# A fill by load instead of a memset, and one late store shared by two queues, in a sparse attention and ELU feed-forward kernel

## The chip, the core and the metric

The kernel runs on one core of one Trainium2 chip. A core has TensorE (PE in the profile; its weight loads are PEld), VectorE (DVE), ScalarE (ACT), GpSimd (POOL) and SyncE (SP), and 16 DMA engines. Each engine works through its own list of instructions in order, and waits at an instruction until the semaphores that this one names have been reached. SP, ScalarE and GpSimd also issue DMAs. The metric is the device time of one execution in microseconds; the median of three runs of the kernel before is 307.64 us (307.57 to 308.14).

## The reference, cut to what matters

Eight batches of eight heads of 576 tokens with 64 dimensions go through masked attention; four heads have a local mask (the last 32 tokens), four a strided one (tokens at the same place modulo 32). The result, 4608 tokens of 512 features, goes through a feed-forward part with an ELU between its two products.

```python
scores = scale * np.matmul(q, k.transpose(0, 1, 3, 2))
mask_local = (rel >= 0) & (rel < stride)                       # stride = 32
mask_strided = (rel >= 0) & (pos[None, :] % stride == pos[:, None] % stride)
masks = np.stack([mask_local if h < H // 2 else mask_strided for h in range(H)], axis=0)
scores = np.where(masks[None, :, :, :], scores, -1000000000.0)
attn = np.exp(scores - np.max(scores, axis=-1, keepdims=True))
attn = attn / (np.sum(attn, axis=-1, keepdims=True) + 1e-09)
x = np.matmul(attn, v).transpose(0, 2, 1, 3).reshape(B * S, H * D)   # 4608 x 512
h = x @ w_in                                                         # 512 -> 2048
g = np.where(h > 0.0, h, np.exp(np.minimum(h, 0.0)) - 1.0)
out = g @ w_out                                                      # 2048 -> 512
```

## The kernel before, in words

Tokens are handled in a permuted order: 576 tokens are 72 places by 8 phases, so both masks become small blocks. Attention works by pairs of heads: a pair is named by batch, kind (`s` strided, `l` local) and a number, as in `0l1`. Its steps are the products of scores (`S`, L450), the exponential on ScalarE (`e`, L457), the multiplication with the mask on VectorE (`m`, L464 for strided and L470 for local pairs), the products with the values (`O`), the logarithm and the reciprocal of the sums on ScalarE (`n`, L548, and `r`, L553), and the product that writes the normalised result, transposed, into `xT` (`x`, L578, VectorE).

The feed-forward part works on nine chunks of 512 tokens. For each chunk there are 16 tiles of the first product (`L`, or its halves `a` and `b`, L605), each followed by an exponential on ScalarE (`h`, L613), a clamp (`i` on VectorE, L622, or `j` on ScalarE, L620) and the step that forms the ELU (`g`, VectorE, L633 or L631). Then four output tiles of 128 tokens follow: their products (`Z`, L639, in four parts), a copy from PSUM to SBUF (`o` on ScalarE or `q` on VectorE, L645) and the store (`t`, L657).

All of this is written out by hand: the string `ORDER` lists every step as a token, and each engine and each DMA queue gets its instructions in this order. `D` tokens issue loads from GpSimd's queue (`D.ql.3` the local queries of batch 3, `D.wo0.0` a quarter of the second weight matrix); `X` tokens issue transposing DMAs from SP's queue; `F.mk` and `F.ml` make the local mask. `w` tokens are products of zeros that fill TensorE's gaps in the first 20 us.

Around the first edit: `F.mk` runs on GpSimd two selections that form `mask_1` (L340, L343), and then the memset of rows 64 to 79 of the tile `ql1` (L346). `F.ml` runs on VectorE two copies that spread `mask_1` into the two halves of `mask_l` (L349), and a small memset (L351). In `ORDER` the tokens between and behind them are, in the neighbourhood: `F.mk r.0s0.0 ... D.wo0.0 F.ml e.0l1.0 ... c.0l0.k n.0s0.1 D.wo1.0 ... m.0l1.0 ... r.0s1.1 ... x.0s1.1 ... V.0`. Here `c.0l0.k` is the copy of transposed keys on VectorE (L426), `V.0` a copy within the value tile (L582).

`ql1` is the second buffer of the local queries; batches 3, 5 and 7 load it, 72 rows each, four loads (L239, one per head). A transposing DMA (L598) reads it in blocks of 80 rows, so its rows 72 to 79 are read too, although no product uses what comes of them. The first buffer, `ql`, has its 80 rows filled by the load of batch 0.

Around the second edit: the last tokens of `ORDER` finish chunks 8 and 7. A tile of 128 tokens is stored in two or three DMAs, because its rows cross the phase blocks in `out`. `store` takes a list of engines, SP alone by default, and its DMAs go to them by turns. The last tile (`Y` and `y` tokens, L669 and L679) is computed and stored in three pieces of 256, 128 and 128 columns; the first piece's two DMAs go from SP, those of the other two from SP and ScalarE by turns. The built program gives DMAs eight completion semaphores for the loads of GpSimd's queue and eight for the DMAs of SP's and ScalarE's queues together, and uses them in turn; a DMA's issue waits until the DMA before it on its semaphore has landed, unless an earlier wait says so already.

Of the kernel before, what the change touches and what calls it, by code (L numbers as in the profile page):

```python
# [17 lines left out]
HG = 4  # L18
NS = 8
RS = S // NS  # L20
RP = 80
# [9 lines left out]
NPE = 2  # L31
# [109 lines left out]
i.7.14 g.7.14 Z.7.2.0.6 h.7.4 i.8.8 j.7.8 Z.8.2.0.7 g.8.8 g.7.8 j.7.4 Z.8.0.0.4 g.8.10 L.8.15.1 g.7.4  # L141
Z.8.3.1.2 h.8.15 i.8.15 Z.8.0.1.4 g.8.15 Z.8.2.1.7 Z.8.1.0.5 Z.7.2.1.6 Z.8.1.1.5 Z.7.1.0.3 Z.8.1.2.5
Z.8.0.2.4 Z.7.2.2.6 Z.8.1.3.5 Z.8.0.3.4 o.8.1 Z.7.0.1.0 o.8.0 t.8.0 Z.8.3.2.2 Z.7.1.1.3 t.8.1 Z.7.1.2.3
Z.8.3.3.2 Z.7.2.3.6 o.8.3 t.8.3 Z.7.0.2.0 q.7.2 Z.7.1.3.3 t.7.2 Z.7.0.3.0 q.7.1 Z.8.2.2.7 t.7.1 q.7.0
Z.8.2.3.7 t.7.0 Y.7.3.0.6 o.8.2 t.8.2 y.7.3.0 Y.7.3.1.5 y.7.3.1 Y.7.3.2.4 y.7.3.2
"""

# [2 lines left out]
def kernel(  # L150
# [9 lines left out]
    nc = tc.nc  # L160
# [20 lines left out]
    g = [consts.tile([128, MC, CHUNK], BF16, tag=f"g{i}", name=f"g{i}") for i in range(2)]  # L181
# [10 lines left out]
    odd = {"ql": consts.tile([RP, HG * NS * D], BF16, tag="ql1", name="ql1"),  # L192
           "kl": consts.tile([LQ, HG * LB * D], BF16, tag="kl1", name="kl1")}
# [25 lines left out]
    def rawof(nm, b):  # L219
        if b == 1:  # L220
            return raw1[nm]
        return odd[nm] if b % 2 and nm in odd else raw[nm]

    def runs(x, b, h, n):

        rows = RP if (b * H + h + n - 1) * S + RP * NS <= B * H * S else RS
        return rows, bass.AP(x.tensor, x.offset + (b * H + h) * S * D,
                             [[NS * D, rows], [S * D, n], [1, NS * D]])
# [5 lines left out]
            out=rawof(nm, b)[0:rows].rearrange("p (h f) -> p h f", h=HG)[:, h0:h0 + n], in_=in_)  # L234

    def load_qloc(b):
        t = rawof("ql", b).rearrange("p (y s x d) -> p y s x d", y=2, s=NS, x=2)
        for h in range(HG):
            nc.gpsimd.dma_start(  # L239
                out=t[0:RS, h % 2, :, h // 2, :],  # L240
                in_=q[b, h].rearrange("(p s) d -> p s d", s=NS))
# [21 lines left out]
    def load(what, b, y=None):  # L263
        nm, b = what[:2], int(b)
        if y is not None:
            load_runs(nm, b, 2 * int(y), 2)
            return
        if nm == "wi":
            i = int(what[2])
            nc.gpsimd.dma_start(out=w_in_sb[:, :, i * 512:(i + 1) * 512],  # L270
                                in_=w_in_v[:, :, i * 512:(i + 1) * 512])
        elif nm == "wo":
            i = int(what[2])
            nc.gpsimd.dma_start(out=w_out_sb[:, i * 4:(i + 1) * 4, :],
                                in_=w_out_v[:, i * 4:(i + 1) * 4, :])
        elif nm == "vl":
            load_vloc(b)
        elif nm == "ql" and b >= NPE:
            load_qloc(b)
        elif nm == "kl" and b >= NPE:  # L280
            load_kloc(b)
        else:
            load_runs(nm, b)
# [5 lines left out]
    for eng, n, x in ((nc.sync, 0, q), (nc.scalar, 1, k)):  # L289
        for i in range(2):  # L290
            rows, in_ = runs(x, 0, HG, 2)
            f = NS * D // 2
            eng.dma_start(out=half(stage[0:rows, n * 4 * f:(n + 1) * 4 * f], i),
                          in_=in_[:, :, i * f:(i + 1) * f])
# [14 lines left out]
    def fill_ones(t, n):  # L309
        w = t.bitcast(F32)  # L310
        nc.vector.memset(
            w[:, 0:n * D].rearrange("p (n w d) -> p n w d", w=2, d=D // 2)[:, :, 0, :], two)
        nc.vector.memset(w[:, n * D:], two)

    def fill_vloc(t):
        fill_ones(t, HG * LB)
        nc.vector.memset(blocks(t, HG * LB)[0:PRE, 0, :], 0.0)
# [10 lines left out]
    def fill(what):  # L328
        if what == "ms":
            nc.vector.tensor_scalar(same, dist, scalar1=STRIDE // NS - 1, scalar2=None,  # L330
                                    op0=ALU.bitwise_and)
            nc.vector.tensor_scalar(eq, same, scalar1=0, scalar2=None, op0=ALU.is_equal)
            nc.vector.scalar_tensor_tensor(mask_s, dist, float(RS), eq, op0=ALU.is_ge,
                                           op1=ALU.mult)
        elif what == "vp":
            fill_ones(vs_p, HG * NS)
        elif what == "v1":
            fill_vloc(vl_t[1])
        elif what == "mk":
            nc.gpsimd.affine_select(  # L340
                mask_1, mask_1, compare_op=ALU.is_ge, fill=0.0,
                base=-1, pattern=[[-1, NS], [-NS, LN]], channel_multiplier=1)
            nc.gpsimd.affine_select(  # L343
                mask_1, mask_1, compare_op=ALU.is_ge, fill=0.0,
                base=PRE, pattern=[[1, NS], [NS, LN]], channel_multiplier=-1)
            nc.gpsimd.memset(odd["ql"][64:RP], 0.0)  # L346
        else:
            for u in range(2):
                nc.vector.tensor_copy(mask_l[:, u],  # L349
                                      mask_1.unsqueeze(2).to_broadcast([128, NS, 3, LN]))  # L350
            nc.vector.memset(mask_l[0:PRE, 0, :, 0, :], 0.0)  # L351
# [263 lines left out]
    def clamp(eng, ch, m):  # L615
        i = int(ch), int(m)
        e = tiles.pop(("he", i))
        e1 = p_he1.tile([128, CHUNK], BF16, tag="he1", name="he1")
        if eng is nc.scalar:
            nc.scalar.activation(e1, e, ACT.Relu, bias=1.0, scale=-1.0)  # L620
        else:
            eng.tensor_scalar(e1, e, scalar1=1.0, scalar2=1.0, op0=ALU.min, op1=ALU.subtract)  # L622
        tiles["he1", i] = (e1, eng is nc.scalar)
# [19 lines left out]
    def copy_o(eng, ch, kk):  # L643
        o_sb = tiles["osb", ch, kk] = p_osb.tile([128, d_model], F32, tag="osb", name="osb")
        eng(o_sb, tiles.pop(("o", int(ch), int(kk))))  # L645
# [3 lines left out]
    def store(ch, kk, engs=(nc.sync,), fs=slice(0, d_model)):  # L649
        o_sb = tiles["osb", ch, kk]  # L650
        c0 = int(ch) * CHUNK + int(kk) * 128
        c, i = c0, 0
        while c < c0 + 128:
            b, r = divmod(c, S)
            s, p = divmod(r, RS)
            n = min(RS - p, c0 + 128 - c)
            engs[i % len(engs)].dma_start(out=out_v[b, s, p:p + n, fs], in_=o_sb[c - c0:c - c0 + n, fs])  # L657
            c, i = c + n, i + 1
# [15 lines left out]
    def out_piece(ch, kk, i):  # L674
# [8 lines left out]
    run = {  # L683
        "w": warm, "K": lambda nm, x: cast(nc.vector.tensor_copy if nm == "q" else nc.scalar.copy, nm, x),
        "k": lambda nm, x: cast(nc.scalar.copy if nm == "q" else nc.vector.tensor_copy, nm, x), "T": transposes, "F": fill,
        "c": lambda *a: copy_T(nc.vector.tensor_copy, *a),
        "C": lambda *a: copy_T(nc.scalar.copy, *a),
# [2 lines left out]
        "a": lambda ch, m, bk: l1(ch, m, (2, 3), bk), "b": lambda ch, m: l1(ch, m, (0, 1)),  # L690
        "L": lambda ch, m, bk: l1(ch, m, (2, 3, 0, 1), bk), "h": exp_h,
        "i": lambda *a: clamp(nc.vector, *a), "j": lambda *a: clamp(nc.scalar, *a),
        "g": elu, "Z": l2, "t": store, "Y": l2_piece, "y": out_piece,
        "o": lambda *a: copy_o(nc.scalar.copy, *a),
        "q": lambda *a: copy_o(nc.vector.tensor_copy, *a),
    }
# [33 lines left out]
```

## Time and profile before

| | us |
|---|---|
| median of three runs | 307.64 |
| the profiled execution, as a whole | 308.06 |
| its span, from the first to the last instruction | 306.3 |
| TensorE busy (matmul) | 294.3 |
| VectorE busy | 227.3 |
| ScalarE busy | 228.6 |
| GpSimd busy | 81.7 |

The granted TensorE clock was 0.998 on the mean. The lines that follow below are taken from one execution. A line of a timeline gives the start, the duration, the engine, the line of the kernel, the operation, what it writes and reads, its shape and how many like it were merged; in brackets stands how long the engine had been idle before it, and what ended that. A line of the chain gives start, duration and what held the end of the kernel up in that time. A line of a group by source line gives least, median and greatest duration in ns. A line of waits gives who waited for what, the total in us, how often, and the longest. An engine's name with a q behind it is its queue, where DMAs are issued and semaphores are waited for.

### The profile page before, as it was taken

The page shows a single profiled execution, that of the slowest core. Times are in us where ns is not written, and L with a number is a line of the kernel's source. Part 1 is how long each engine was busy: PE and PEld are TensorE (multiplying, and loading weights), DVE is VectorE, ACT ScalarE, POOL GpSimd, SP SyncE. Part 2 cuts the span into 40 slices and gives each one's busy share as a digit, 9 for nine tenths or more (in the row PEclk, how much of TensorE's full clock was granted, in tenths as well). Part 3 has the DMA queues.
Part 4 walks back from the last instruction along what each step waited for, and adds up shares of the span by engine and source line. Part 5 has one row for each costly group of instructions (what it writes and reads, how often), then busy time and mean ns, then how long its engine had stood idle before and what let it go on. Part 6 is the DMA issues. An engine that isn't in the chain of part 4 may idle for free.

```text
span 306.3 us, 6219 instructions
## 1 busy us (share of the span) xinstructions
PE 294.3 (96%) x2299; PEld 146.8 (48%) x2339; DVE 227.3 (74%) x435; ACT 228.6 (75%) x412; POOL 81.7 (27%) x110
## 2 busy tenths in 40 slices
PE   6999999999999999999999999999999999999993
PEld 2654455445544454545544554454444544444453
DVE  6877959798779978896788878976788468894020
ACT  4778678588879888997989889978786659881110
POOL 8943336630472008530178240000000000000000
PEclk9999999999999999999999999999999999999999
DMA  8999999999999859999899599601120022000143
GB/s 164 184 206 206 207 193 166 153 196 207 169 153 168 127 118 134 162 193 159 203 149 155 65 138 167 166 26 46 37 68 0 2 68 68 2 1 0 28 150 98
DMA packets 107278, 37.59 MB, mean 123 GB/s; under 512 B 89104, under 2 KB 102768, under 8 KB 107248
## 3 DMA queue, kind: packets, MB, share of 16 engines
q0 software_dynamic: 69648, 19.43, 62.9%
q1 hardware_dynamic: 37088, 17.38, 27.8%
q10 hardware_dynamic: 512, 0.39, 0.5%
q8 instruction: 18, 0.29, 0.4%
q14 instruction: 12, 0.10, 0.1%
HBM read 39.47 MB, written 9.44 MB: 160 GB/s over the span
## 4 chain that ended last, share of the span: by engine, by line
PE 86%; DVE 6%; ACT 2%; issue 2%; DMA 2%; ACTq 0%; DVEq 0%
PE ps L639 39%; PE ps L605 36%; PE ps L450 3%; DVE g L633 2%; PE ps L520 2%; PE ps L513 2%; DVE he L622 2%; DMA g<-in_k_dram 2%; PE ps L669 1%; ACT he L613 1%; DVE mask_l L349 1%; DVE xT L578 1%; PE ps L493 0%; ACT e L457 0%; PE ps L408 0%
## 5 line engine op out<-in xcount | busy, mean ns | idle before, releaser
L639 PE MATMUL ps<-w_out_sb,g 128*128 128x512 bf16 x538 | 129.6, 379 | 2.0 <-issue 0.6
L605 PE MATMUL ps<-xT,w_in_sb 128*128 128x512 bf16 x559 | 129.4, 379 | 1.6 <-issue 0.3
L613 ACT ACTIVATE he<-ps 128x512 f32<-128x512 f32 x144 | 81.0, 597 | 22.2 <-PE ps L605 19.9
L605 PEld LDWEIGHTS <-w_in_sb 128*128 128x128 bf16 x576 | 55.0, 98 | 64.9 <-issue 1.7
L639 PEld LDWEIGHTS <-g 128*128 128x128 bf16 x560 | 51.1, 98 | 55.6 <-issue 0.6
L633 DVE TENSOR_TENSOR g<-he,ps 128x512 bf16<-128x512 bf16 x92 | 62.0, 684 | 1.9
L578 DVE TENSOR_TENSOR xT<-ps,ln 64x576 bf16<-64x576 f32 (+1 forms) x64 | 42.5, 677 | 19.7 <-ACT ln L553 18.9
L457 ACT ACTIVATE e<-ps 72x576 bf16<-72x576 f32 (+1 forms) x64 | 39.1, 647 | 13.4 <-PE ps L450 11.7
L622 DVE TENSOR_SCALAR he<-he 128x512 bf16<-128x512 f32 x92 | 40.1, 445 | 7.7 <-ACT he L613 7.0
L548 ACT ACTIVATE ln<-ps 64x576 f32<-64x576 f32 (+1 forms) x64 | 36.3, 583 | 9.8 <-PE ps L520 4.9
L631 DVE SCALAR_TENSOR_TENSOR g<-he,ps 128x512 bf16<-128x512 bf16 x52 | 34.8, 682 | 7.2 <-ACT he L620 6.9
L553 ACT ACTIVATE ln<-ln 64x576 f32<-64x576 f32 (+1 forms) x64 | 38.5, 619 | 1.2
L620 ACT ACTIVATE he<-he 128x512 bf16<-128x512 f32 x52 | 32.5, 630 | 1.6 <-DVE g L633 1.1
L645 DVE COPY osb<-ps 128x512 f32<-128x512 f32 x22 | 15.1, 685 | 16.3 <-PE ps L639 16.0
L239 POOL DMA_DIRECT2D ql<-in_q_dram x24 | 19.9, 833 | 6.8 <-DMA vl<-in_v_dram 3.1
L645 ACT COPY osb<-ps 128x512 f32<-128x512 f32 x13 | 7.6, 586 | 18.0 <-PE ps L639 14.1
L246 POOL DMA_DIRECT2D kl<-in_k_dram x24 | 17.8, 745 | 11.9 <-DMA w_out_sb<-in_moe_w_out_dram 4.0
L470 DVE TENSOR_TENSOR pm<-e,mask_l 128x576 bf16<-128x576 bf16 x32 | 14.1, 454 | 7.0 <-ACT e L457 5.4
L464 DVE TENSOR_TENSOR pm<-e,mask_s 72x576 bf16<-72x576 bf16 x32 | 14.2, 450 | 4.3 <-ACT e L457 4.1
L233 POOL DMA_DIRECT2D vs<-in_v_dram x8 | 5.2, 653 | 26.4 <-DVE vsp L585 25.2
L256 POOL DMA_DIRECT2D vl<-in_v_dram x8 | 9.6, 1195 | 8.7 <-PE ps L520 6.4
L513 PEld LDWEIGHTS <-vsp 72*128 72x128 bf16 x192 | 9.1, 98 | 5.4 <-DVE pm L464 0.3
(93 smaller groups left out, 156.1 us busy)
## 6 DMA issues: line engine op xcount, KB each, us to landing
out_dram<-osb SPq DMA_DIRECT2D x32, 144.0 KB
vl<-in_v_dram POOLq DMA_DIRECT2D x8, 288.0 KB, 8.8
w_in_sb<-in_moe_w_in_dram POOLq DMA_DIRECT2D x4, 512.0 KB, 13.0
w_out_sb<-in_moe_w_out_dram POOLq DMA_DIRECT2D x4, 512.0 KB, 16.3
kl<-in_k_dram POOLq DMA_DIRECT2D x24, 72.0 KB, 7.7
ql<-in_q_dram POOLq DMA_DIRECT2D x24, 72.0 KB, 8.8
ks<-in_k_dram POOLq DMA_DIRECT2D x5, 320.0 KB, 8.4
vs<-in_v_dram POOLq DMA_DIRECT2D x5, 320.0 KB, 8.6
```

Of the source, the lines that this page charges most:

```text
L457: nc.scalar.activation(e[0:R], tiles.pop(("S", key, u))[0:R], ACT.Exp, scale=scale)
L548: nc.scalar.activation(t, s_ps, ACT.Ln)
L553: nc.scalar.activation(t, t, ACT.Exp, scale=-1.0)
L578: nc.vector.tensor_mul(dst, o_ps, rc)
L605: nc.tensor.matmul(tiles["h", ch, m], lhsT=w_in_sb[:, c, m * 128:(m + 1) * 128], rhs=xT[:, c, ch * CHUNK:(ch + 1) * CHUNK], start=(c == 2) ...
L613: nc.scalar.activation(e, tiles["h", i[0], i[1]], ACT.Exp)
L620: nc.scalar.activation(e1, e, ACT.Relu, bias=1.0, scale=-1.0)
L622: eng.tensor_scalar(e1, e, scalar1=1.0, scalar2=1.0, op0=ALU.min, op1=ALU.subtract)
L631: nc.vector.scalar_tensor_tensor(dst, e1, -1.0, h, op0=ALU.mult, op1=ALU.max)
L633: nc.vector.tensor_tensor(dst, e1, h, op=ALU.max)
L639: nc.tensor.matmul(ops, lhsT=g[ch % 2][:, m, kk * 128:(kk + 1) * 128], rhs=w_out_sb[:, m, :], start=(m == 0), stop=(m == MC - 1), skip_gro ...
L645: eng(o_sb, tiles.pop(("o", int(ch), int(kk))))
```

## The change

The memset of `ql1` is taken out of `F.mk`. In its place the loads of `D.ql.3` begin with one more load, of eight rows by four heads from the query tensor (2 KB of float32 each), into rows 72 to 79 of `ql1`; batches 5 and 7 find them filled. Tile 8.3 is stored with the new token `u`, which gives the store SP and ScalarE by turns: its first DMA (56 rows) goes from SP, its second (72 rows) from ScalarE.

```diff
@@ -141,7 +141,7 @@
 i.7.14 g.7.14 Z.7.2.0.6 h.7.4 i.8.8 j.7.8 Z.8.2.0.7 g.8.8 g.7.8 j.7.4 Z.8.0.0.4 g.8.10 L.8.15.1 g.7.4
 Z.8.3.1.2 h.8.15 i.8.15 Z.8.0.1.4 g.8.15 Z.8.2.1.7 Z.8.1.0.5 Z.7.2.1.6 Z.8.1.1.5 Z.7.1.0.3 Z.8.1.2.5
 Z.8.0.2.4 Z.7.2.2.6 Z.8.1.3.5 Z.8.0.3.4 o.8.1 Z.7.0.1.0 o.8.0 t.8.0 Z.8.3.2.2 Z.7.1.1.3 t.8.1 Z.7.1.2.3
-Z.8.3.3.2 Z.7.2.3.6 o.8.3 t.8.3 Z.7.0.2.0 q.7.2 Z.7.1.3.3 t.7.2 Z.7.0.3.0 q.7.1 Z.8.2.2.7 t.7.1 q.7.0
+Z.8.3.3.2 Z.7.2.3.6 o.8.3 u.8.3 Z.7.0.2.0 q.7.2 Z.7.1.3.3 t.7.2 Z.7.0.3.0 q.7.1 Z.8.2.2.7 t.7.1 q.7.0
 Z.8.2.3.7 t.7.0 Y.7.3.0.6 o.8.2 t.8.2 y.7.3.0 Y.7.3.1.5 y.7.3.1 Y.7.3.2.4 y.7.3.2
 """
 
@@ -234,6 +234,10 @@
             out=rawof(nm, b)[0:rows].rearrange("p (h f) -> p h f", h=HG)[:, h0:h0 + n], in_=in_)
 
     def load_qloc(b):
+        if b == NPE + 1:
+            nc.gpsimd.dma_start(
+                out=odd["ql"][RS:RP].rearrange("p (h f) -> p h f", h=HG),
+                in_=runs(q, b, 0, HG)[1][RS:RP])
         t = rawof("ql", b).rearrange("p (y s x d) -> p y s x d", y=2, s=NS, x=2)
         for h in range(HG):
             nc.gpsimd.dma_start(
@@ -343,7 +347,6 @@
             nc.gpsimd.affine_select(
                 mask_1, mask_1, compare_op=ALU.is_ge, fill=0.0,
                 base=PRE, pattern=[[1, NS], [NS, LN]], channel_multiplier=-1)
-            nc.gpsimd.memset(odd["ql"][64:RP], 0.0)
         else:
             for u in range(2):
                 nc.vector.tensor_copy(mask_l[:, u],
@@ -690,7 +693,8 @@
         "a": lambda ch, m, bk: l1(ch, m, (2, 3), bk), "b": lambda ch, m: l1(ch, m, (0, 1)),
         "L": lambda ch, m, bk: l1(ch, m, (2, 3, 0, 1), bk), "h": exp_h,
         "i": lambda *a: clamp(nc.vector, *a), "j": lambda *a: clamp(nc.scalar, *a),
-        "g": elu, "Z": l2, "t": store, "Y": l2_piece, "y": out_piece,
+        "g": elu, "Z": l2, "t": store,
+        "u": lambda ch, kk: store(ch, kk, (nc.sync, nc.scalar)), "Y": l2_piece, "y": out_piece,
         "o": lambda *a: copy_o(nc.scalar.copy, *a),
         "q": lambda *a: copy_o(nc.vector.tensor_copy, *a),
     }
```

`runs(q, b, 0, HG)` is the address pattern of the strided tiles: 80 rows of 512 elements for each of four heads. Of these the new load takes rows 72 to 79.

## The prediction

> **What bounds the kernel now.** I read the page's head and its chain first, then the chain by time in the two stretches where the edits sit (12 to 24 us and the last 20 us), then the timelines of single engines there, and last the waits of SP's queue.
>
> ```profile
> span 306.3 us, 6219 instructions
> PE 294.3 (96%) x2299; PEld 146.8 (48%) x2339; DVE 227.3 (74%) x435; ACT 228.6 (75%) x412; POOL 81.7 (27%) x110
> PE 86%; DVE 6%; ACT 2%; issue 2%; DMA 2%; ACTq 0%; DVEq 0%
> ```
>
> TensorE sets the pace for 86% of the chain, so an edit counts only where the chain leaves TensorE. It does so at the start (attention of batch 0) and behind the last matmul. Both edits touch exactly these places. The chain at the start, by time:
>
> ```profile
> 12.84 0.46 DVE xT L578
> 13.30 1.60 DVE mask_l L349 x2
> ...
> 15.53 0.45 DVE pm L470
> ...
> 22.70 0.74 DVE he L622
> 23.46 0.70 DVE g L633
> 24.20 0.38 PE ps L605
> ```
>
> VectorE, not TensorE, is the chain from 12.8 to 17.4 us, and its largest piece is the pair of copies that spreads the local mask (L349).
>
> **Edit 1, the memset removed.** The two mask copies have one shape, yet one took 165 ns and the other 1595. Beside the long one stands the memset on GpSimd that the change removes:
>
> ```profile
> L349 DVE COPY mask_l<-mask x2: 165/880/1595, 13.2 to 14.7; 128x288 bf16<-128x288 bf16 x2
> 12.92 1.80 POOL L346 MEMSET ql<- 16x2048 bf16 x1
> 14.90 0.70 DVE L426 COPY kTl<-ps 128x576 bf16<-128x576 bf16 x1
> 14.67 1.50 POOL L274 DMA_DIRECT2D w_out_sb<-in_moe_w_out_dram  x2
> ```
>
> The long copy, the first, runs from 13.2 to 14.8 (13.2 + 1.595) and the memset to 14.72 (12.92 + 1.80): the copy ends some 0.1 us behind the memset. The other copy, behind the memset, takes 0.165. So I read 1595 - 165 = 1430 ns of the long copy as waiting for the memset. The Trainium skill, page "SBUF — State Buffer", section "SBUF: two separate sides", says that VectorE's two-port copies and GpSimd share a port pair which the first to start keeps for its whole instruction; these rows agree with that.
>
> Without the memset the copies end near 13.47 (13.30 + 0.165), the key copy L426 moves from 14.90 to about 13.5. Not all of the 1.43 us arrives, for ScalarE is late next:
>
> ```profile
> 14.77 0.43 ACT L553 ACTIVATE ln<-ln 128x288 f32<-128x288 f32 x1
> 15.89 0.45 DVE L578 TENSOR_TENSOR xT<-ps,ln 128x288 bf16<-128x288 f32 x1
> PE ps L450 <- DVE kTl L426: 0.5, 1, 0.5
> ```
>
> L578 at 15.89 needs the reciprocal that ScalarE ends at 14.77 + 0.43 = 15.20, and that one hangs on TensorE products that the edit doesn't move. So L578 can start at 15.23 (the same 0.03 us as between neighbours in the chain), a gain of 15.89 - 15.23 = 0.66 us. VectorE then has 0.6 us to spare ahead of it: L426, the mask product L470 (0.45) and the copies are done by 14.65. TensorE's wait of 0.5 us for L426 goes too. Everything behind, to the first products of the feed-forward part, hangs on VectorE and ScalarE in turn and moves by the same 0.66.
>
> What issues in the memset's place are the two weight loads L274, from 12.9 instead of 14.67. They meet the mask copies. The second copy ran at 14.74 inside such an issue (14.67 to 15.42) and took 165 ns, so I take no delay. The other end comes from a clamp inside another issue:
>
> ```profile
> DMA  8999999999999859999899599601120022000143
> 22.45 0.75 POOL L274 DMA_DIRECT2D w_out_sb<-in_moe_w_out_dram  x1 [2.78 <-DMA w_in_sb<-in_moe_w_in_dram]
> 22.70 0.73 DVE L622 TENSOR_SCALAR he<-he 128x512 bf16<-128x512 f32 x1 [0.73 <-ACT he L613]
> L622 DVE TENSOR_SCALAR he<-he x92: 405/421/983, 22.7 to 278.8; 128x512 bf16<-128x512 f32 x92
> ```
>
> The clamp took 0.73 where the median is 0.42: 0.31 us late. Two such delays, 0.62, would use up the 0.6 us of room and no more.
>
> By the skill's rule (same page and section: the pair is kept for the whole instruction, and descriptor generation on GpSimd needs it) both issues would hold the copies to about 14.45, L426 would end near 15.25, and edit 1 would bring some 0.3 us less. The rows speak against so long a hold: one copy passed inside an issue unhindered, and the clamp ended 0.23 us after its issue, less than its own length.
>
> The same clamp gives a second gain. It is on the chain (22.70 above), and the issue it met is timed by a landing of w_in_sb, which I take as unmoved: the page's DMA row is at 9 tenths there, and GpSimd's queue has work outstanding before and after, so loads issued 1.8 us earlier only wait longer. With everything 0.66 us earlier, the clamp runs from 22.04 to 22.46 and is through when the issue starts at 22.45. That is another 0.73 - 0.42 = 0.31, so 0.97 us by the product at 24.20. If the two still meet, 0.66 stays.
>
> Does TensorE then run into a load? The tightest is the third slice of w_in_sb, whose landing released that issue (just before 22.45); its first use:
>
> ```profile
> 23.43 0.60 PE L605 MATMUL ps<-xT,w_in_sb 128*128 128x512 bf16 x2
> ```
>
> 0.66 earlier is 22.77, still behind 22.45. The later loads have more room. So the head gives 0.97, with ends of 0.3 (L274 in the memset's place, clamp still met) and 1.43 + 0.31 = 1.74 (ScalarE not late).
>
> **Edit 1, the load added.** In batch 3 the new 8-row load is queued on GpSimd ahead of the four of ql:
>
> ```profile
> 60.79 0.83 POOL L239 DMA_DIRECT2D ql<-in_q_dram  x1 [0.43 <-issue]
> 64.78 0.80 POOL L239 DMA_DIRECT2D ql<-in_q_dram  x1 [0.43 <-DMA ks<-in_k_dram]
> 80.56 0.67 POOL L233 DMA_DIRECT2D qs<-in_q_dram  x1 [14.98 <-DMA out_dram<-osb]
> 80.84 1.73 SPq L598 DMA_TRANSPOSE qTl<-ql  x1
> ```
>
> It costs GpSimd one issue of some 0.65 us (like L233 here, 0.67). Since loads count completions on eight semaphores in turn, every later load now waits for its neighbour's predecessor; the fourth ql load waits for a landing about 2 us later than now. Behind it GpSimd has 15 us idle (14.98 above), and the transpose of ql on SP's queue, which gains one more load to wait for, is issued at 80.84, 16 us behind the last ql load. That hides the load; without that cover it would cost its 0.65. What isn't hidden by it is VectorE: clamps meet GpSimd issues in this stretch, and here the chain is VectorE's:
>
> ```profile
> 57.19 0.99 DVE he L622
> 60.80 1.06 DVE he L622 x2
> ```
>
> The first lost 983 - 421 = 0.56 us, the pair some 0.3 (1.06 against 0.42 + 0.34, the step between neighbours). The issues keep their times (landings), the clamps come about 1 us earlier, so the collisions are drawn anew. Before had 0.86 us of them; after may have none or as much again. I take zero, with -0.86 and +0.86 as ends.
>
> **Edit 2, one store by turns.** Tile 8.3 is stored in two pieces, both now from SP, the second at 293.77; this one goes to ScalarE. SP next waits for VectorE's copy anyway, and ScalarE idles:
>
> ```profile
> 293.77 0.37 SPq L657 DMA_DIRECT2D out_dram<-osb  x1
> 293.66 0.69 DVE L645 COPY osb<-ps 128x512 f32<-128x512 f32 x1 [13.76 <-PE ps L639]
> 298.02 0.59 ACT L645 COPY osb<-ps 128x512 f32<-128x512 f32 x1 [4.64 <-PE ps L639]
> ```
>
> So the issue saved (0.37) is worth nothing by itself, and the one on ScalarE (0.54 by the row below) is hidden in 4.64 us of idle time; were that gone, it would delay the last copies by 0.54. But the stores of SP and ScalarE count on eight semaphores too, in turn over both queues, and a store waits for the one before it on its semaphore. The order of SP's and ScalarE's stores in the built program changes this turn. The last stores now:
>
> ```profile
> 298.21 0.34 SPq L657 DMA_DIRECT2D out_dram<-osb  x1
> 297.94 3.55 PE ps L669 x48
> 300.62 0.29 DVE L679 COPY osb<-ps 128x128 f32<-128x128 f32 x1 [3.67 <-PE ps L669]
> 301.51 0.29 DVE osb L679
> 300.94 0.54 ACTq L657 DMA_DIRECT2D out_dram<-osb  x1
> SPq L657 <- DMA out_dram<-osb: 1.7, 1, 1.7
> 303.00 0.47 SPq L657 DMA_DIRECT2D out_dram<-osb  x1
> 303.57 0.54 SPq L657 DMA_DIRECT2D out_dram<-osb  x1
> ```
>
> The last tile's second piece (copied by 300.62 + 0.29 = 300.91) is split between ScalarE, at 300.94, and SP. In the program of before both halves have the same semaphore, ScalarE's first: SP stands 1.7 us until ScalarE's store has landed (300.94 to about 302.95), issues its half at 303.00, and the third piece's half, ready since 301.51 + 0.29 = 301.80, only at 303.57. In the changed program the second piece's SP half waits for a store of tile 7.0 (issued at 298.21 and long landed), and can go at about 301.3. Now the third piece's SP half shares a semaphore with ScalarE's half of the second piece. It goes at about 303.00, where its forerunner went. The last issue moves from 303.57 to 303.00, and the 2.73 us behind it (landing and the program's end, 306.30 - 303.57) follow: 0.57 us gained. Two transfers beside each other may slow ScalarE's landing; bounds: 0 (it slips 0.57) and 0.57 + 1.2 (the third piece goes right after its copy at 301.80).
>
> **The sum.** 0.97 + 0 + 0.57 = 1.54 us. The profiled execution took 308.06 around its span of 306.3; 308.06 - 1.54 = 306.5. It lay 0.42 above the median of the runs, 307.64, so I forecast 306.1 for the median.
>
> **Rivals.** *Head only* (306.7): the store moved between queues brings nothing, because ScalarE's landing slips by as much or SP's wait stays with the second piece. The Trainium skill, page "DMA: Bandwidth & Descriptors", section "Issuing engines are not separate DMA queues", says that issuing from several engines saves only the sequencer's issue time. Here that time is free, which gives this rival. For it: SP's 0.6 us of idle time behind 293.77. Against: the 1.7 us wait, which is neither transfer nor issue.
>
> *Tail only* (307.1): the head's gain is lost on the way, in new collisions like that at 57.19 (0.56 and 0.30 more on the chain than now) or at a landing. For it: loads land when they land. Against: the one tight landing, 22.45, is still ahead of 22.77.
>
> *Neither* (307.6): the edits move nothing; the long copy would need another cause than the memset.
>
> *Slower* (308.3 or more): the longer run of GpSimd issues between 56 and 67 us meets the clamps harder. Each meeting costs up to 0.56; it takes four more on the chain (2.24 - 1.54 = +0.7 us) to pass 308.26, the bound of slower. In before two of the clamps met there on the chain, in the whole kernel few of 92 (the median is 421).
>
> **How the numbers follow.** Forecast 0.60, head only 0.16, tail only 0.12, neither 0.04, slower 0.08. About 0.2% (0.6 us) is what a measurement of this kernel can tell from no change. Faster: 0.60 + 0.16 = 0.76; the same: 0.12 + 0.04 = 0.16; slower 0.08. The range goes from 306.1 - 0.86 = 305.2 (no collisions left) to 307.2 (tail only); it leaves out the last two cases and a little of the rest.
>
> **What would show it.** Right: both mask copies near 165 ns and at about 13.2, ScalarE's L553 ahead of L578 as the wait; L578 at 15.2; no TensorE wait for L426; the product of 24.20 near 23.2; at the end SP's 1.7 us wait ahead of the last store, not the one before it. Wrong: a mask copy still over 1 us; the same wait at the same store; or clamps (L622) with more ends over 700 ns between 55 and 66 us on the chain.

## The result, and the profile after

The changed kernel took 306.38 us (median, 305.72 to 306.66) against 307.44 (307.17 to 308.14) for the kernel before, both over six runs. The ratio is 0.9957, with a 95% interval of 0.9945 to 0.9970: 1.06 us of median, faster by more than the 0.2% that can be told from no change. The forecast was 306.1. The profiled execution took 306.37 around its span of 304.7; that of before took 308.06 around 306.3.

In the changed kernel a line number lies 3 to 4 higher (L349 is now L352, L426 L429, L553 L556, L578 L581, L605 L608, L622 L625, L657 L660, L669 L672); in the kernels of the experiments it shifts likewise by a few lines. First the page's head and the engines' shares of the chain that ended last:

```profile
span 304.7 us, 6218 instructions
PE 293.7 (96%) x2299; PEld 146.7 (48%) x2339; DVE 225.7 (74%) x435; ACT 228.4 (75%) x412; POOL 80.7 (26%) x110
PE 88%; DVE 3%; ACT 3%; issue 3%; DMA 2%; ACTq 0%; DVEq 0%
```

VectorE's share of the chain has halved, from 6% to 3%; TensorE has 88%, before 86%. The head of the kernel, from the group of the two mask copies and from the timelines of VectorE, GpSimd and TensorE (start, duration, engine, line; in brackets the idle time before and what ended it):

```profile
L352 DVE COPY mask_l<-mask x2: 165/274/383, 13.2 to 13.5; 128x288 bf16<-128x288 bf16 x2
13.67 0.70 DVE L429 COPY kTl<-ps 128x576 bf16<-128x576 bf16 x1
15.21 0.46 DVE L581 TENSOR_TENSOR xT<-ps,ln 128x288 bf16<-128x288 f32 x1 [0.47 <-ACT ln L556]
12.79 1.50 POOL L278 DMA_DIRECT2D w_out_sb<-in_moe_w_out_dram  x2
15.04 0.30 PE L453 MATMUL ps<-qTl,kTl 64*128 64x96 bf16 x6
22.03 0.43 DVE L625 TENSOR_SCALAR he<-he 128x512 bf16<-128x512 f32 x1 [0.73 <-ACT he L616]
22.18 0.75 POOL L278 DMA_DIRECT2D w_out_sb<-in_moe_w_out_dram  x1 [2.19 <-DMA w_in_sb<-in_moe_w_in_dram]
```

The long copy of 1595 ns is gone; the longer one now takes 383, inside the first of the two weight loads that moved into the memset's place. The key copy runs at 13.67 instead of 14.90, and the product that waited 0.5 us for it starts at 15.04 instead of 15.66, without a wait. L581 starts at 15.21 and is now held by ScalarE's reciprocal (0.47). The clamp is through by 22.46 and takes 0.43, where it took 0.73 at 22.70.

The end, from the chain by time, the waits of SP's queue and its timeline:

```profile
296.85 3.55 PE ps L672 x48
SPq L660 <- DMA out_dram<-osb: 1.1, 1, 1.1
299.85 0.54 ACTq L660 DMA_DIRECT2D out_dram<-osb  x1
300.24 0.54 SPq L660 DMA_DIRECT2D out_dram<-osb  x1
301.92 0.47 SPq L660 DMA_DIRECT2D out_dram<-osb  x1
```

TensorE's last product ends at 300.40 (296.85 + 3.55) instead of 301.49 (297.94 + 3.55), 1.09 us earlier. SP issues the second piece's half at 300.24, 0.1 us behind the end of its issue before that (300.14) and without a wait for a landing; it waits for one only ahead of the last store, which goes at 301.92, once ScalarE's store of 299.85 has landed. From the last product to that issue it is now 1.52 us, before 2.08 (303.57 - 301.49).

Followed through both traces, the products stand thus against before: 0.62 us earlier at 15.66, 0.97 at 24.20, 0.77 at 38.5, 0.99 at 62.6, 1.36 at 66.1, 0.98 at 99 and 1.09 at the end. TensorE's gain is made in the first 24 us; what follows only swings around it.

### The profile page after: what moved, and what is told of

Same layout as the page of the kernel before. It is cut to its first block, busy times and chain, and to the rows that moved or that the text cites. A ratio compares the mean times of both kernels' runs of the same rounds, so it can differ in the third digit from the quotient of the medians.

```text
span 304.7 us, 6218 instructions
## 1 busy us (share of the span) xinstructions
PE 293.7 (96%) x2299; PEld 146.7 (48%) x2339; DVE 225.7 (74%) x435; ACT 228.4 (75%) x412; POOL 80.7 (26%) x110
## 3 DMA queue, kind: packets, MB, share of 16 engines
q0 software_dynamic: 69728, 19.47, 62.6%
## 4 chain that ended last, share of the span: by engine, by line
PE 88%; DVE 3%; ACT 3%; issue 3%; DMA 2%; ACTq 0%; DVEq 0%
PE ps L642 40%; PE ps L608 37%; PE ps L453 3%; PE ps L523 2%; PE ps L516 2%; DMA g<-in_k_dram 2%; PE ps L672 1%; DVE g L636 1%; DVE he L625 1%; PE ps L411 1%; ACT he L616 1%; PE ps L385 1%; ACT ln L551 1%; PE ps L496 0%; ACT e L460 0%
## 5 line engine op out<-in xcount | busy, mean ns | idle before, releaser
L608 PE MATMUL ps<-xT,w_in_sb 128*128 128x512 bf16 x559 | 129.1, 379 | 1.1 <-issue 0.3
L608 PEld LDWEIGHTS <-w_in_sb 128*128 128x128 bf16 x576 | 55.0, 98 | 64.1 <-issue 0.9
L581 DVE TENSOR_TENSOR xT<-ps,ln 64x576 bf16<-64x576 f32 (+1 forms) x64 | 42.6, 678 | 20.2 <-ACT ln L556 19.4
L625 DVE TENSOR_SCALAR he<-he 128x512 bf16<-128x512 f32 x92 | 39.6, 439 | 7.6 <-ACT he L616 7.0
L556 ACT ACTIVATE ln<-ln 64x576 f32<-64x576 f32 (+1 forms) x64 | 38.5, 619 | 1.2
```

The lines of the kernel that those rows point to most:

```text
L556: nc.scalar.activation(t, t, ACT.Exp, scale=-1.0)
L581: nc.vector.tensor_mul(dst, o_ps, rc)
L608: nc.tensor.matmul(tiles["h", ch, m], lhsT=w_in_sb[:, c, m * 128:(m + 1) * 128], rhs=xT[:, c, ch * CHUNK:(ch + 1) * CHUNK], start=(c == 2) ...
```

## The experiments

Two theories stood against each other for the head: that the memset *holds* VectorE's copy, so that it is the memset's place in time that counts; or that something else on GpSimd or in the loads changed and moved the copy. For the tail: that the gain comes from which semaphore a store gets; or that it comes from the issue saved on SP's queue. All times are of whole executions: medians, or a single execution where the table says so. Each ratio is to executions of the kernel before that were made beside it (medians of 307.44 to 307.53). TensorE's end is that of the last product's own record in the profiled execution (some 0.02 us ahead of the end of its piece in the chain), "behind it" what follows to the span's end.

| kernel | us | ratio to before (95%) | TensorE's end | behind it |
|---|---|---|---|---|
| before | 307.44 | | 301.48 | 4.87 |
| changed | 306.38 | 0.9957 (0.9945 to 0.9970) | 300.38 | 4.28 |
| first edit alone | 306.79 | 0.9977 (0.9967 to 0.9987) | 300.20 | 4.89 |
| second edit alone | 306.96 | 0.9985 (0.9976 to 0.9993) | 301.00 | 4.25 |
| memset later | 306.61 | one execution | 299.97 | 4.89 |
| load added, memset kept | 307.42 | 1.0002 (0.9991 to 1.0013) | 300.69 | 4.86 |
| mask copies as maxima | 307.42 | one execution | 300.82 | 4.88 |
| half of the memset in place | 307.02 | one execution | 300.42 | 4.88 |
| two stores by turns | 305.77 | 0.9938 (0.9926 to 0.9951) | 300.48 | 3.87 |
| first edit, second piece from SP | 306.63 | one execution | 300.83 | 4.09 |
| changed, again | 306.19 | 0.9959 (0.9945 to 0.9972) | 300.12 | 4.26 |
| two stores by turns, again | 306.19 | 0.9956 (0.9941 to 0.9972) | 299.90 | 3.87 |
| before, again | 307.34 | one execution | 300.75 | 4.88 |

### The first edit alone

The changed kernel with the old store:

```diff
-... o.8.3 u.8.3 Z.7.0.2.0 ...
+... o.8.3 t.8.3 Z.7.0.2.0 ...
```

> The first edit alone: the memset is gone and the small load of batch 3 is there, the store of tile 8.3 stays on SP. Theory (the memset held up the mask copies, and the store's gain comes from the semaphore turn): mask copies under 0.4 us each, TensorE's product of 24.20 about 0.97 us earlier, TensorE's last product about 1.1 us earlier, the 1.7 us wait on SP's queue as in before, time 0.9 to 1.2 us under before. Rival (the changed kernel's gain is mostly that of the store): within 0.4 us of before.

It brings 0.23% (0.71 us of 307.5): less than the 0.9 to 1.2 expected, more than the rival's 0.4. The mask copies take 383 and 165 ns as in the changed kernel, the product of 24.20 comes 0.95 us earlier, TensorE ends at 300.20 (1.28 earlier than in the profile of before), and at the end SP stands as it did before:

```profile
SPq L660 <- DMA out_dram<-osb: 1.7, 1, 1.7
```

### The second edit alone

```diff
-... o.8.3 t.8.3 Z.7.0.2.0 ...
+... o.8.3 u.8.3 Z.7.0.2.0 ...
+        "u": lambda ch, kk: store(ch, kk, (nc.sync, nc.scalar)),
```

> The second edit alone: tile 8.3 is stored from SP and ScalarE, the memset stays. Theory: TensorE's end unmoved, SP's wait for ScalarE's landing stands ahead of the last store and not of the one before it, from TensorE's last product to the end 0.5 to 0.6 us less, time 0.57 us under before. Rival (moving a store saves issue time only, and that time is free here): no change, within 0.2 us.

It brings 0.15% (0.46 us; 0.57 expected). From the groups, the waits and the timelines:

```profile
L349 DVE COPY mask_l<-mask x2: 166/881/1596, 13.1 to 14.6; 128x288 bf16<-128x288 bf16 x2
SPq L657 <- DMA out_dram<-osb: 1.1, 1, 1.1
22.62 0.43 DVE L622 TENSOR_SCALAR he<-he 128x512 bf16<-128x512 f32 x1 [0.75 <-ACT he L613]
22.43 0.92 POOL L274 DMA_DIRECT2D w_out_sb<-in_moe_w_out_dram  x1 [2.42 <-DMA w_in_sb<-in_moe_w_in_dram]
```

The long copy stays, SP's wait is the short one, and what lies behind the last product falls from 4.87 to 4.25 us. Both edits alone add up to 1.17 us, which lies inside the interval of both together (0.3% to 0.55% of 307.5, so 0.92 to 1.69 us). TensorE's end was expected unmoved and came 0.48 us earlier. The last two rows speak against a step of the prediction: with the memset in place, the first clamp took 0.43, not 0.73. It did start inside the issue of the weight load, 0.19 us behind its start, and was not held.

### The memset at another time

The kernel before, with the memset moved in GpSimd's queue behind the third load of batch 1; nothing else is changed.

```diff
-            nc.gpsimd.memset(odd["ql"][64:RP], 0.0)          # in F.mk
+        elif what == "mq":
+            nc.gpsimd.memset(odd["ql"][64:RP], 0.0)
-... D.ks.1 n.0l0.0
+... D.ks.1 F.mq n.0l0.0
```

> Before, with the memset kept and only moved in GpSimd's queue from ahead of the first loads of w_out to behind the third load of batch 1 (about 18 us), where VectorE runs no copy within SBUF. No added load, no moved store. Theory (the memset matters by where it stands beside VectorE's copies): mask copies under 0.4 us, the product of 24.20 about 0.97 us earlier as in the changed kernel; span about 305.2. Rival (the gain needs GpSimd to be relieved of the 1.8 us): the product at 24.20 moves by under 0.3 us.

```profile
L350 DVE COPY mask_l<-mask x2: 165/274/384, 13.1 to 13.4; 128x288 bf16<-128x288 bf16 x2
18.39 1.80 POOL L336 MEMSET ql<- 16x2048 bf16 x1
```

The same memset, as long as before, costs nothing at 18.39: the copies are as short as in the changed kernel, the product of 24.20 comes 1.10 us earlier (0.97 expected), TensorE ends at 299.97 and the execution took 306.61. It is the meeting that costs, not the memset.

### The load without the rest

The changed kernel with the old store and with the memset put back; the load stays.

```diff
-... o.8.3 u.8.3 ...
+... o.8.3 t.8.3 ...
+            nc.gpsimd.memset(odd["ql"][64:RP], 0.0)          # in F.mk
```

> Before, with the small load of batch 3 added and the memset kept: the price of the load by itself. Theory: it is hidden in GpSimd's idle time and redraws some meetings of VectorE's clamps with GpSimd's issues between 56 and 67 us; TensorE's last product within 0.5 us of before either way, the first clamp and the mask copy as in before. Rival (the load costs what its issue takes on GpSimd and its landing): 0.65 us or more slower.

```profile
60.44 0.57 POOL L238 DMA_DIRECT2D ql<-in_q_dram  x1
66.74 0.81 POOL L243 DMA_DIRECT2D ql<-in_q_dram  x1 [1.33 <-DMA vl<-in_v_dram]
```

The ratio of 1.0002 says that the load costs nothing that these runs can tell. It takes 0.57 us of GpSimd; the fourth load of ql comes at 66.74 instead of 64.78, and the transpose that reads it goes only at 81.26. Two expectations were missed: TensorE's last product came 0.79 us earlier than in the profile of before (within 0.5 was expected), and the first clamp took 0.43 where it was expected as in before. It started at 22.73, inside the issue of the weight load (22.14 to 22.89) but only 0.16 us ahead of its end.

### Another form for the mask copies

The memset stays in place; the copies are written as the maximum of the mask with itself, which gives the same values by an instruction with two inputs.

```diff
-                nc.vector.tensor_copy(mask_l[:, u],
-                                      mask_1.unsqueeze(2).to_broadcast([128, NS, 3, LN]))
+                m3 = mask_1.unsqueeze(2).to_broadcast([128, NS, 3, LN])
+                nc.vector.tensor_tensor(mask_l[:, u], m3, m3, op=ALU.max)
```

> Before, memset kept in its place; only the two mask copies are written as the maximum of the mask with itself, an instruction with two inputs in SBUF (as the mask products, 0.45 us for 576 elements) in place of a copy with one. Theory (the long copy waits because its form needs what the memset holds): no instruction of 1.6 us, two of 0.2 to 0.5 us beside the memset, the key copy starts at 13.7 to 14.2, TensorE's product of 15.66 about 0.5 to 0.6 us earlier. Rival (anything on VectorE there waits for the memset to end, by a semaphore or by the port): the first still ends at 14.8.

```profile
13.07 0.52 DVE L350 TENSOR_TENSOR mask_l<-mask 128x288 bf16<-128x288 bf16 x2
12.78 1.80 POOL L346 MEMSET ql<- 16x2048 bf16 x1
15.09 0.46 DVE L578 TENSOR_TENSOR xT<-ps,ln 128x288 bf16<-128x288 f32 x1 [0.46 <-ACT ln L553]
...
159.32 1.11 DVE L622 TENSOR_SCALAR he<-he 128x512 bf16<-128x512 f32 x1
158.95 1.25 POOL L256 DMA_DIRECT2D vl<-in_v_dram  x1
```

Both maxima run in 0.52 us in the middle of the memset and are through by 13.59, while it runs to 14.58. So a copy is held beside the memset and a maximum of the same shape is not: it is not the data, the mask's readiness or a semaphore. Nor is it that the weight loads come earlier without the memset, for here they still go at 14.52. At the head this kernel gains as much as the changed one (L578 at 15.09, the product of 15.66 0.75 us earlier). In its one execution the gain is not to be seen at the end: 307.42 against 307.44, with TensorE's end at 300.82. The last two rows show where it went: a clamp on the chain, held beside a GpSimd DMA issue, takes 1.11 us where 0.42 is usual (1109 ns, the longest of all profiles), and TensorE's lead over before falls from 1.28 us at 156.9 to 0.64 at 161.7.

### Half of the memset

```diff
-            nc.gpsimd.memset(odd["ql"][64:RP], 0.0)          # in F.mk
+            nc.gpsimd.memset(odd["ql"][64:RP, 0:HG * NS * D // 2], 0.0)
+        elif what == "mq":                                   # behind D.ks.1
+            nc.gpsimd.memset(odd["ql"][64:RP, HG * NS * D // 2:], 0.0)
```

> Before with half of the memset (1024 of 2048 columns) in its old place and the other half behind the third load of batch 1. Theory: the first mask copy ends about 0.1 us behind the first half, which takes some 0.9 us (12.92 to 13.85), so it lasts 0.7 us instead of 1.6, and since VectorE has 0.6 us of room ahead of ScalarE's reciprocal at 15.2, TensorE's product of 15.66 moves by the full 0.6 us as without any memset. Rival (the gain goes with the memset's length): product of 15.66 moves by about 0.3 us.

```profile
L351 DVE COPY mask_l<-mask x2: 165/454/743, 13.3 to 13.9; 128x288 bf16<-128x288 bf16 x2
12.96 0.94 POOL L348 MEMSET ql<- 16x1024 bf16 x1
```

The half memset ends at 13.90 and the copy at some 14.0: as before, the copy ends 0.1 us behind the memset, wherever that ends. The product of 15.66 comes 0.56 us earlier, near the full 0.6 of the theory and not the rival's 0.3. Together with the maxima and the late memset this shows the mechanism that the prediction read from one pair of rows.

### Two stores by turns

If a store's semaphore makes the wait, the wait must be removable without taking any transfer away. The changed kernel with tile 7.2 by turns too:

```diff
-... Z.7.1.3.3 t.7.2 Z.7.0.3.0 ...
+... Z.7.1.3.3 u.7.2 Z.7.0.3.0 ...
```

> The changed kernel with tile 7.2 stored by turns as well (its second DMA from ScalarE). By the built program no late store of SP then shares a semaphore with a late store of ScalarE just ahead of it. Theory (the semaphore turn sets the end): no wait of SP for a landing behind TensorE's end, the last two stores go right after VectorE's last copy (0.35 us behind TensorE's last product, in before 2.1), from TensorE's last product to the end 3.1 us instead of 4.8 in before and 4.3 in the changed kernel; time about 1.1 us under the changed kernel, 2.3 under before. Rival (only issue time is saved): at most 0.37 us under the changed kernel.

```profile
296.95 3.55 PE ps L672 x48
300.34 0.54 SPq L660 DMA_DIRECT2D out_dram<-osb  x1
300.98 0.55 SPq L660 DMA_DIRECT2D out_dram<-osb  x1
300.84 0.47 ACTq L660 DMA_DIRECT2D out_dram<-osb  x1
SPq L729 <- DMA out_dram<-osb: 0.9, 2, 0.6
```

None of these stores waits for a landing any more; the last one goes at 300.98, 0.48 us behind the last product (300.50) where it was 1.52 in the changed kernel. Of these 1.04 us only 0.4 arrive: 3.87 us lie behind the last product instead of 4.28, and about 3.1 were expected. The last issue no longer sets the end. Behind it SP's closing instructions (L729) wait for the landings of ScalarE's last two stores (issued at 299.95 and 300.84); some 0.4 us there wait for nothing that the profile shows. In the first set of runs this kernel took 305.77, 0.6 us under the 306.38 of the changed kernel where 1.1 were expected.

### The second piece from SP

The first edit alone, with the second piece of the last tile stored by SP only:

```diff
-        store(ch, kk, (nc.sync,) if i == "0" else (nc.sync, nc.scalar), slice(f0, f1))
+        store(ch, kk, (nc.sync, nc.scalar) if i == "2" else (nc.sync,), slice(f0, f1))
```

> The first edit alone (8.3 on SP), and of the last tile the second piece stored wholly from SP, so that ScalarE issues one store only. Theory: SP never waits for a landing of ScalarE's; it issues four stores back to back behind the first piece's copy and the last one about 0.9 us behind TensorE's last product; from there to the end 3.6 us, though SP issues one store more than in before. Rival (issue time counts): one issue more on SP, 0.5 us more than the first edit alone.

SP's last store:

```profile
301.97 0.70 SPq L660 DMA_DIRECT2D out_dram<-osb  x1
```

This *adds* an issue to SP's queue and takes one from ScalarE's, the opposite of what the second edit does, and still 4.09 us lie behind the last product instead of 4.89: SP never stands for a landing ahead of a store, and the last issue goes at 301.97 (TensorE's end 300.83). So it is the turn of the semaphores that pays, not the issue saved. The size was missed here too (3.6 expected).

### Changed kernel, two stores and before, once more

> The changed kernel once more, beside the next two on one chip. The theory by now (head 0.6 to 0.7 us by the mask copies, end 0.57 by the semaphore turn, and meetings of clamps with GpSimd's issues that fall differently in each execution): 1.0 to 1.4 us under before, the product of 24.20 about 0.65 us earlier than in an execution of before whose first clamp is not met.

> The changed kernel with tile 7.2 stored by turns as well, once more. From TensorE's last product to the end 3.9 us against 4.3 in the changed kernel; time 0.4 us under the changed kernel, 1.5 to 1.9 under before.

> The kernel before, a second profile. If the meeting of the first clamp with the issue of the w_out load (22.70) is chance, as the second edit alone and the load with the memset kept suggest, it can be missing here: the clamp near 0.42 us and the product of 24.20 at about 23.9; the mask copy still 1.6 us and the 1.7 us wait on SP's queue still there. If it belongs to the kernel, the clamp takes 0.7 us again.

Side by side on one chip, the changed kernel and the one with two stores by turns both took 306.19. Behind the last product the second has again 3.87 us and the first 4.26, but this 0.4 us is as large as the scatter of what comes ahead, and no gain in time is shown: the 0.4 us under the changed kernel and the 1.5 to 1.9 under before (it was 1.34) were missed. The changed kernel's ratio repeats (0.9959), 1.34 us under before. Its product of 24.20 lies 0.64 us ahead of that with the load added and the memset kept, whose first clamp wasn't held and whose memset started as in before; 0.65 was expected.

The kernel before, profiled again, shows what belongs to the kernel and what to one execution:

```profile
13.25 1.80 POOL L346 MEMSET ql<- 16x2048 bf16 x1
13.22 2.00 DVE L349 COPY mask_l<-mask 128x288 bf16<-128x288 bf16 x2
21.82 0.75 POOL L274 DMA_DIRECT2D w_out_sb<-in_moe_w_out_dram  x1 [1.71 <-DMA w_in_sb<-in_moe_w_in_dram]
23.03 0.43 DVE L622 TENSOR_SCALAR he<-he 128x512 bf16<-128x512 f32 x1 [0.73 <-ACT he L613]
```

The long copy is there again, longer still because the memset started later (the first of the two copies took 1916 ns and ended 0.09 us behind the memset). By these rows it started 0.03 us ahead of the memset and was held all the same. The meeting of the first clamp with the weight load isn't there: the landing that releases the load came 0.63 us earlier (21.82 against 22.45), the clamp 0.33 later. TensorE's products of this execution stand against the first one of the *same* kernel 0.33 us later at 15.66, level at 24.20 (at 24.23, where 23.9 was expected: the later memset took back what the clamp gave), 0.69 earlier at 66.1 and 0.72 earlier at the end.

## Why the prediction was right, and where a term was off

**The head, 0.66: right.** L581 starts at 15.21 (15.23 forecast), held by ScalarE's reciprocal as forecast; the product at 15.66 is 0.62 earlier. The mechanism is shown by three runs (maxima, late memset, half memset). In time, over the four profiles with the full memset ahead of the copies TensorE ends on the mean at 300.98 (301.48, 301.00, 300.69, 300.75), over the nine others at 300.35: 0.63 us, though the two groups overlap (300.69 to 301.48, 299.90 to 300.83). The first edit alone brought 0.71 us of median.

**The mask copies near 165 ns: wrong for the first of them.** It takes 383 ns, and 536 when the changed kernel was profiled again. The weight load in the memset's place, inside whose issue it starts, is what can have held it; no run tested that by itself. The prediction took no delay from the one copy that passed, and kept 0.6 us of room for two delays. The room covers it: L429 is 1.23 us earlier, not 1.4, and L581 still waits for ScalarE. By the Trainium skill (page "SBUF — State Buffer", section "SBUF: two separate sides") the first to start keeps the shared pair; the half memset agrees (the copy ends 0.1 us behind it). In before again the rows show the copy first by 0.03 us, and yet it was the one that was held: there the trace doesn't bear out the order of starts. Nor does an issue keep the copies to its end: both were through by 13.66, with the second issue running to 14.29.

**The first clamp, 0.31: the mis-sized term.** The sum took this meeting as a property of the kernel that the edit removes. It was a chance of the profiled execution: with the memset in place the clamp took 0.43 in the three other profiles (22.62 with the second edit alone, 22.73 with the load added, 23.03 in before again), and of all thirteen profiles it was held in this one alone. In two of those three it started inside the issue as well, once near its start and once near its end, where it isn't held (last section). The pair of traces does show 0.97 at 24.20, as forecast, but only because the profile of before held the bad draw. The typical gain there is nothing, which makes the sum 0.66 + 0 + 0.57 = 1.23 us and the forecast 307.64 - 1.23 = 306.4; measured 306.38. That this agrees so well is partly luck, for the runs of before beside the changed kernel had a median of 307.44: the gain to compare is 1.06 us. The prediction's own remark that this execution lay 0.42 us above the median was the hint: a part of that 0.42 was most likely this term, and it was counted as gain once more.

**The landing taken as unmoved: not so, without harm.** In the changed kernel that weight load goes at 22.18, in before again at 21.82, and the third load of batch 1 goes later than before (17.31):

```profile
17.78 0.64 POOL L233 DMA_DIRECT2D xT<-in_k_dram  x1 [2.75 <-DMA w_in_sb<-in_moe_w_in_dram]
```

**The load added, 0 with ends of 0.86: right.** The load by itself costs nothing that shows (1.0002). The clamps' meetings were drawn anew, as forecast. In the changed profile the chain between 54 and 63 us is TensorE's alone:

```profile
54.03 9.28 PE ps L608 x43
```

The products are 0.99 us earlier at 62.6 and 1.36 at 66.1, yet 1.09 at the end. So those 0.86 us of before were avoided in this execution, but not as net gain; what took most of it again was not followed up. No clamp of the changed kernel is over 744 ns.

**The store, 0.57: right in place and size.** The second piece's half was forecast at about 301.3 and the third's at 303.00; they went at 300.24 and 301.92, which with the 1.09 us of the head added back is 301.33 and 303.01. What lies behind the last product falls by 0.59 (4.87 to 4.28). That this saving is the semaphore's and not the issue's is shown by the piece stored from SP alone. One row was misread: behind 293.77 SP idles for 0.24 us (294.14 to 294.38), not 0.6; its next store waits for VectorE's copy all the same, so the saved issue stays worth nothing. The Trainium skill (page "DMA: Bandwidth & Descriptors", section "Issuing engines are not separate DMA queues") leaves to several issuing engines only the issue time; here 0.6 us came from moving a store to another engine because it shifted whose landing the next store waits for.

**The rivals.** *Head only* and *tail only* both fall, as each edit brings its own part (0.71 and 0.46 us). *Neither* falls with the mask copies. *Slower* falls: the longer run of issues in batch 3 cost nothing that shows.

What stays open: which meeting costs or saves how much between 24 us and the end. Two executions of one kernel differ there by up to 0.7 us; only the clamp of 1109 ns in the kernel with the maxima could be followed to TensorE (0.64 us).

## What to carry to other kernels

A long instruction beside a copy of the same shape that runs ten times faster can point at a neighbour that holds it: look which engine's instruction ends just ahead of it, and try moving that one, or write the copy in a form that isn't held (here the maximum). Before a delay of a few tenths is counted as a gain, ask whether its cause repeats in every execution (an order of instructions does) or hangs on a landing (this one moved by 0.6 us); if the profiled execution lies above the median, the excess may be such delays, and taking them out of the sum again counts them twice. At the end of a kernel follow the semaphores of the last stores in both queues: a wait there can be for the landing of another queue's store, and moving a store ahead of it can shift that wait, until the closing landings set the end.

## What the runs showed of the hardware

**A GpSimd DMA issue holds a clamp only in its middle part.** Taken over all thirteen profiles, 310 clamps started inside a GpSimd DMA issue. All 107 that started within its first 0.24 us took their normal 0.41 to 0.43 us. Of the 203 that started later, 103 took over 0.05 us longer, and all of these ended as if they had started 0.16 to 0.20 us ahead of the issue's end; the mean loss was 0.20 us, the largest 0.69. Of the 100 that weren't held, 88 started in the issue's last 0.24 us; the other 12 started 0.66 to 0.79 us ahead of the end of issues of 0.92 to 1.25 us. The timelines of VectorE and GpSimd in the changed kernel have both kinds within one issue:

```profile
27.08 0.95 DVE L625 TENSOR_SCALAR he<-he 128x512 bf16<-128x512 f32 x2
27.04 0.75 POOL L278 DMA_DIRECT2D w_out_sb<-in_moe_w_out_dram  x1 [1.90 <-DMA w_in_sb<-in_moe_w_in_dram]
```

The first clamp starts 0.04 us into the issue and takes 0.42. The second starts 0.37 into it, takes 0.61 and ends at 28.03, 0.24 behind the issue's end (27.79). The mask copies go much the same way: 13.19 lies 0.4 into its issue (383 ns); in the changed kernel's second profile the copy starts 0.25 in (536 ns), and both end as if they had started 0.14 us ahead of the issue's end; in before, the second copy 0.06 in (165 ns). That the prediction saw one copy pass and one clamp held was thus no contradiction. In both profiles of two stores by turns the copies, started 0.09 and 0.24 us in, took 234 to 235 and 226 to 227 ns; these 0.06 to 0.07 us over 165 are not explained.

**One execution to the next**, the same kernel's chain shifts by 0.7 us at nearly the same clock (0.996 and 0.998 granted in the two profiles of before; the slower execution had the higher one): as much as either edit is worth. At 24.20 the two are level, the first clamp's 0.31 us and the later memset's 0.33 having cancelled, so the 0.7 us arises behind it; that it comes of such meetings is likely, but not shown.
